# A mixed attention and state-space kernel: two power tables, three chunk-state buffers, parked queries and larger rings for VectorE's exps

## The chip, the cores and the metric

The kernel runs on one core of a Trainium2 chip. The metric is the device time of one execution in microseconds. One execution was also profiled. PE is TensorE, DVE is VectorE, ACT is ScalarE, POOL is GpSimd and SP is SyncE, which here issues nearly all the DMAs.

## What is computed

S = 2048 positions, D = 512 channels, 32 heads of 16. `a` is softmax attention over x, `b` is a state-space convolution of the same input x, and a sigmoid gate mixes the two.

```python
def _A_ref(x, wqkv, wo):
    qkv = (x @ wqkv).reshape(B, S, 3, H, Dh).transpose(2, 0, 3, 1, 4)
    q, k, v = qkv[0], qkv[1], qkv[2]
    p = softmax(einsum("bhqd,bhkd->bhqk", q, k) * Dh ** -0.5)
    return einsum("bhqk,bhkd->bhqd", p, v).transpose(0, 2, 1, 3).reshape(B, S, D) @ wo

def _B_ref(u, A_re, A_im, B_re, B_im, C_re, C_im, log_dt, Dskip):
    dt = exp(log_dt)[:, None]
    P = exp((dt * (A_re + 1j * A_im))[:, :, None] * arange(L))
    K = einsum("dn,dnl,dn->dl", C_re + 1j * C_im, P, dt * (B_re + 1j * B_im)).real
    return causal_convolution(u, K) + u * Dskip        # written with FFTs in the reference

g = sigmoid((x * gate_w).sum(-1, keepdims=True))
out = g * _A_ref(x, wqkv, wo) + (1 - g) * _B_ref(x, ...)
```

The kernel represents each channel's state-space part by powers of one complex number and works in chunks of 64 positions: a power table, the effect within a chunk, the state that a chunk leaves, a scan over chunks, and the output from the states.

## The kernel before

A planner in Python (`record`) writes out the instructions of all five engines. The operations are grouped in generators, called threads (`first`, `projs`, `table`, `scan` and so on), each with a priority; a smaller number goes first. A thread yields operations, or a condition: `AFTER` a mark, `Q` a tile number, or `LOCK` the PSUM bank MB. The planner has a cost for each operation, and at each step it emits what is ready by these costs. On the chip every engine then runs its list in order, with semaphores for dependences. The whole is recorded once, the SBUF addresses are chosen from the first and last use of each buffer (`place`), and the list is emitted.

**Attention** sets the beat. There are 2048 slices of 128 keys by 512 queries of one head, three to a *tile*, so 683 tiles. `fill(t)` is three PE matmuls that write scores into one of two PSUM buffers, SC0 and SC1 (line 572, as all matmuls). `ex(t)` is the exp of a tile on ScalarE (line 725), from PSUM into a ring in SBUF: EX and ET for tiles below TL = 340, EL (9 entries) from there on. `pv` multiplies the exps with the values into the PSUM bank OA; a block of 16 such steps (b, one of 32) ends with `norm` (lines 826 to 832: transpose, reciprocal, product, transpose). Blocks 0 to 7 use the query buffer Q0, 8 to 15 Q1, and so on; `mk_qm` (line 681) makes the masked queries Qm of a block. Matmuls on `wm` keep TensorE's clock up.

**Exps on VectorE.** From tile TL on, `dchoose` may take one slice of a tile away from ScalarE, two slices to a group. `dfirst` (line 736) makes the exponent bits, `dpoly` (lines 756 to 760) makes two correction tensors DP and DC with two maskings and two products. `pv` then adds two more matmuls for that slice. ScalarE's instruction of the tile covers 1024 columns instead of 1536. A new group is begun only if a DP/DC buffer is free (ND = 3), if no other thread has VectorE work ready in the time of the next tile, and if VectorE's backlog by the plan is under DPEND = 2.5 us. The last 40 slices have none.

**The state-space part** runs beside it, in 16 blocks of 32 channels, four blocks to a quarter:

- `table` (lines 983 to 1018): for a pair of blocks, VectorE computes powers into PT from B16 and D16, D32, D48 (12 products, 6 sums, 2 copies), and SP stores PT to DRAM (`ptd`). The next pair waits for `K` of the pair before.
- `kstage` (L1036 to L1044): PE products from PT into MB, VectorE puts them into Kst (L1039, L1041), SP stores to `kpd`, mark `K`.
- `qload` and `sstage` (L1026, L1052 to L1070): SP loads the transposed table into Qt (two buffers), PE multiplies with X2 into MB, VectorE scales into Sst (L1064), SP stores to `sd`. Mark `S`.
- `sload` (L1075 to L1090): SP loads a block's chunk states with a transpose into SG0 or SG1, by the quarter's parity. Quarter 1 waits for the mark `sgfree`, quarters 2 and 3 for `yq0` and `yq1`.
- `scan` (L1093 to L1121): 30 steps a quarter on VectorE, each of two products, an add, the sum into G and a cast back into SG.
- `ystage` (L1142 to L1188): 32 units of PE products from SG, Py, Tt and X2 into MB, a VectorE copy into Yst (L1175), a store to `ytd`. `yread` (L1191) loads the result transposed into Yl. `yq` marks a quarter of it. The thread begins after S15.
- `combine`, `outs` (L1229, L1256): the gate on Yl, the output projection in MB, and the final sum `fo` (L1248).

MB is one PSUM bank and is shared by projections, K, S, y and the output projection, so each of these takes the lock. All DMAs named stand in SP's one queue, in program order.

Of the kernel before, what the change touches and what calls it, by code (L numbers as in the profile page):

```python
# [6 lines left out]
FP32 = mybir.dt.float32  # L7
# [24 lines left out]
ND = 3  # L32
TL = 340
NL = 9
WARM = 2.2
DEBT = 2.5
DPEND = 2.5
DW = ((TL, 9999),)
# [338 lines left out]
def declare(nc, es):  # L377
# [7 lines left out]
    for k in range(4):  # L385
        sb(f"Q{k}", 4 * 512)
    sb("Qm", 2 * 512)
# [3 lines left out]
    sb("EL", NL * 1536)  # L391
# [50 lines left out]
    sb("PT", 2 * 2 * CB * T)  # L442
# [8 lines left out]
    sb("G", 2 * 128, FP32)  # L451
    for n in ("s2", "s3"):
        sb(n, 2 * 128, FP32)

    sb("X2", 4 * 32 * 64)

# [4 lines left out]
    for n in ("DP", "DC"):  # L461
        sb(n, ND * 1024)
# [4 lines left out]
    for n, free in (("ptd", NBLK * P * 2 * CB * T), ("sd", D * NCH * 2 * P),  # L467
                    ("kpd", NBLK * P * 8 * P), ("xrd", S * D), ("ytd", D * S)):
        B[n] = Buf(n, "dr", free, BF16)
        B[n].t = nc.dram_tensor("gm_" + n, [free // P, P], BF16)  # L470
# [7 lines left out]
def place(nc, bufs):  # L478

    base, end = (nc.sbuf_base + 31) // 32 * 32, nc.sbuf_usable_end  # L480
    sbs = [b for b in bufs.values() if b.kind == "sb" and b.first is not None]

    size = {b: (b.nbytes() + 31) // 32 * 32 for b in sbs}
    conf = {b: [o for o in sbs if o is not b and o.first <= b.last + 1 and b.first <= o.last + 1] for b in sbs}

    def fit(order):
        over = 0
        for b in sbs:
            b.lo = None
        for b in order:  # L490
            at = base
            for lo, hi in sorted((o.lo, o.lo + size[o]) for o in conf[b] if o.lo is not None):
                if at + size[b] <= lo:
                    break
                at = max(at, hi)
            b.lo, b.hi = at, at + size[b]
            over += max(0, b.hi - end)
        return over

    seed = 1  # L500

    def rnd(n):
        nonlocal seed
        seed = (seed * 1103515245 + 12345) % 2 ** 31
        return (seed >> 8) % n

    first = sorted(sbs, key=lambda b: -(b.last - b.first + 30) * size[b])
    for k in range(24000):
        if k % 4000 == 0:
            order, best = first, None  # L510
        o = list(order)
        if best is not None:
            x = out[rnd(len(out))] if rnd(10) < 6 else o[rnd(len(o))]
            o.remove(x)
            o.insert(rnd(len(o)), x)
        over = fit(o)
        if best is None or over <= best:
            order, best, out = o, over, [b for b in sbs if b.hi > end]
        if best == 0:
            break  # L520
    assert best == 0, (best, live(sbs))
    fit(order)
# [35 lines left out]
def record(p, B, ins):  # L558
# [109 lines left out]
    def proj_ev(kind, idx, c, bank):  # L668
# [5 lines left out]
        o, at, ky = (KT, idx * S + 512 * c, (idx, c)) if kind == "K" else (B[f"Q{c}"], 512 * idx, idx)  # L674
# [35 lines left out]

    def et(t, n):
        if t >= TL:
            b, e = B["EL"], (t - TL) % NL
        else:
            b, e = (B["EX"], t - NE) if NE <= t < NE + NX else (ET, t % NE)
        return b, 1536 * e + 512 * n, (b, (e, n), t)
# [11 lines left out]
    VC, DP, DC = (B[n] for n in ("VC", "DP", "DC"))  # L728
    groups, gof = [], {}

    def dfirst(t, n):
        b, o, ky = et(t, n)
        sc = SC[t % 2]
        if t >= TL + NL:
            yield ("AFTER", ("pv", tiles[t - NL][n] // 4))
# [12 lines left out]
    def dpoly(g):  # L748
        k = g["n"] % ND
# [14 lines left out]
    def dchoose(t, start, end):  # L764
# [5 lines left out]
        if g is None:  # L770
            if not any(lo <= t < hi for lo, hi in DW):
                return
            if len(groups) >= ND and any(tiles[t_][n_] // 4 >= pvn for t_, n_ in groups[-ND]["t"]):
                return
            if any(isinstance(x[3], list) and x[3][0].eng == "DVE" and (p.ready(x[3]) or 0) < end for x in sch.thr if x[0] > 2.6):
                return
            if NS - sl[-1] < 40 or max(p.free["DVE"], start) + sum({.5: .6, 2.6: 1.9}.get(x[0], 0) for x in sch.thr) > start + DPEND:
                return
            g = dict(n=len(groups), t=[], have=0, op1=[])
# [9 lines left out]
    def vcopy():  # L789
        yield ("Q", DW[0][0] - 5)  # L790
# [4 lines left out]
    def pv(q):  # L795
# [4 lines left out]
        for j in range(4):  # L800
# [7 lines left out]
            if dsel.get(t) == n:  # L808
                g = gof[t]
                k = g["n"] % ND  # L810
                o = 1024 * k + 512 * g["pos"][ek]
                vc = lambda: VC(kt * 152 + 34 * pi + 17 * w, [[1, 32]])
                ext = [main, mm(out, ve, lambda: DP(o, [[1, 512]]), rv + [(DP, k, g["n"])], [(OA, 0, b)], False, False, **kw),
                       mm(out, vc, lambda: DC(o, [[1, 512]]), [(VC, 0), (DC, k, g["n"])], [(OA, 0, b)], False, kt == 15, **kw)]
# [165 lines left out]
    PT, Qt, ptd = B["PT"], B["Qt"], B["ptd"]  # L980
    PTN = 2 * CB * T

    def table():
# [5 lines left out]
        for pb in range(NBLK // 2):  # L989
            qr, blks = pb // 2, (2 * pb, 2 * pb + 1)  # L990
            if pb:
                yield ("AFTER", f"K{2 * pb - 1}")
# [4 lines left out]
            for i in range(2):  # L997
                yield [dv(lambda v, i=i, b0=b0, B16=B16: v.tensor_copy(PT(i * PTN, [[CB * T, 2], [T, CB], [1, 16]]),
                                                                       B16(b0 + i * CB * 16, [[2048, 2], [16, CB], [1, 16]])), bk, [W[i]], 1024, 4)]
            for m in range(1, 4):  # L1000
                Dm = B[f"D{16 * m}"]
                for part in range(2):
# [5 lines left out]
                    yield [tt(lambda part=part, m=m: PT(part * CB * T + 16 * m, [[PTN, 2], [T, CB], [1, 16]]),  # L1008
                              lambda: t1(0, [[CB * 16, 2], [16, CB], [1, 16]]), lambda: t2(0, [[CB * 16, 2], [16, CB], [1, 16]]),
                              ALU.add if part else ALU.subtract, [(t1, 0), (t2, 0)], W, 1024, 2)]  # L1010
            for i, blk in enumerate(blks):
                yield [dma("SP", lambda e, i=i, blk=blk: e.dma_start(ptd.dram(blk * P * PTN, [[PTN, P], [1, PTN]]), PT(i * PTN, [[1, PTN]])),
                           [W[i]], [(ptd, blk)], 6.5, .5)]
                sch.mark(f"pt{blk}")
                if blk == 11:
                    sch.mark("sgfree")
# [3 lines left out]
    X2 = B["X2"]  # L1020
# [9 lines left out]
    def kstage(blk):  # L1030
# [3 lines left out]
        o = (blk % 2) * PTN  # L1034
# [15 lines left out]
    def sstage(blk):  # L1050
        q0, qr, bl = (blk % 2) * PTN, blk // 4, blk % 4
        for bank in range(4):  # L1052
            yield ("LOCK", "MB", [(Qt, blk % 2, blk)])
            os = []
            for pp in range(2):
                for j in range(4):
                    k, par = 4 * bank + 2 * pp + j // 2, j % 2
                    os.append(mm(lambda pp=pp, j=j: MB(256 * pp, [[1, 256]], 32 * j, 32),
                                 lambda k=k, par=par: X2(2048 * qr + 16 * bl + k, [[64, 32]], 64 * par, 64),
                                 lambda k=k, par=par: Qt(q0 + 128 * k, [[16 * 128, 2], [1, 128]], 64 * par, 64),  # L1060
                                 [(Qt, blk % 2, blk), (X2, (qr, par))], [(MB, 0, ('S', blk, bank))], pos=(64 * par, 32 * j),
# [11 lines left out]
    SG = [B["SG0"], B["SG1"]]  # L1073

    def sload(blk):  # L1075
        qr, bl = divmod(blk, 4)
        if qr >= 2:
# [448 lines left out]
```

The softmax here doesn't subtract the row's maximum and nothing guards it: scores larger than these inputs give would overflow.

## Time and profile before

| | us |
|---|---|
| median of 4 runs | 905.72 (903.77 to 906.24) |
| profiled execution's own time | 907.96 |
| its span | 906.2 |
| ScalarE busy | 879.1 (97%) |
| TensorE busy, keep-warm matmuls included | 839.3 (93%) |
| VectorE busy | 806.0 (89%) |
| granted TensorE clock, mean | 0.977 |

The profile's groups give line, engine, operation, output and inputs, shapes and count, then busy time and the mean length of one instruction, then the idle time ahead of it with what ended it. Where instructions of one engine overlap, the mean is longer than busy time over count. A window of the trace gives the busy time of each engine between two times, in microseconds from the span's start.

### The profile page before, as it was taken

The page shows a single profiled execution, that of the slowest core. Times are in us where ns is not written, and L with a number is a line of the kernel's source. Part 1 is how long each engine was busy: PE and PEld are TensorE (multiplying, and loading weights), DVE is VectorE, ACT ScalarE, POOL GpSimd, SP SyncE. Part 2 cuts the span into 40 slices and gives each one's busy share as a digit, 9 for nine tenths or more (in the row PEclk, how much of TensorE's full clock was granted, in tenths as well). Part 3 has the DMA queues.
Part 4 walks back from the last instruction along what each step waited for, and adds up shares of the span by engine and source line. Part 5 has one row for each costly group of instructions (what it writes and reads, how often), then busy time and mean ns, then how long its engine had stood idle before and what let it go on. Part 6 is the DMA issues. An engine that isn't in the chain of part 4 may idle for free.

```text
span 906.2 us, 18586 instructions
## 1 busy us (share of the span) xinstructions
PE 839.3 (93%) x7707; PEld 266.7 (29%) x7707; DVE 806.0 (89%) x1684; ACT 879.1 (97%) x693; POOL 10.3 (1%) x18
## 2 busy tenths in 40 slices
PE   7999999888899889898989999999999999999997
PEld 2222222222222222222223333423323332222222
DVE  7999999997477899999999899999898989999972
ACT  6999999999999999999999999999999999999996
POOL 2000000000000000000000000000000000000000
PEclk9999989999999999999999999999899999999999
DMA  8350000007758568787645658664614311000000
GB/s 197 100 94 1 1 1 1 1 1 209 221 146 210 172 156 219 189 214 197 198 100 131 152 107 187 156 134 105 140 39 103 79 26 36 24 1 1 1 1 24
DMA packets 227412, 92.32 MB, mean 102 GB/s; under 512 B 191872, under 2 KB 215040, under 8 KB 225280
## 3 DMA queue, kind: packets, MB, share of 16 engines
q1 hardware_dynamic: 226128, 90.34, 40.6%
q8 instruction: 61, 1.00, 0.5%
q10 hardware_dynamic: 1200, 0.79, 0.3%
q14 instruction: 23, 0.19, 0.1%
HBM read 27.92 MB, written 35.65 MB: 70 GB/s over the span
## 4 chain that ended last, share of the span: by engine, by line
ACT 63%; PE 29%; DVE 6%; issue 1%; POOL 1%; ACTq 0%; DVEq 0%; POOLq 0%
ACT ET L725 37%; ACT EL L725 23%; PE OA L572 15%; PE SC L572 8%; PE MB L572 5%; ACT EX L725 3%; DVE Sst L1064 1%; DVE G L1114 0%; DVE EL L736 0%; DVE s L1108 0%; DVE s L1112 0%; DVE fo L1248 0%; DVE tt L837 0%; DVE s L1110 0%; DVE SG L1116 0%
## 5 line engine op out<-in xcount | busy, mean ns | idle before, releaser
L725 ACT ACTIVATE ET<-SC 128x1536 bf16<-128x1536 f32 x322 | 435.1, 1684 | 5.7 <-PE SC L572 5.5
L725 ACT ACTIVATE EL<-SC 128x1536 bf16<-128x1536 f32 (+1 forms) x343 | 413.0, 1371 | 5.2 <-PE SC L572 3.9
L572 PE MATMUL SC<-Qm,KT 32*128 32x512 bf16 x2048 | 271.2, 390 | 44.4 <-ACT ET L725 20.3
L572 PE MATMUL OA<-wm 128*128 128x512 bf16 x849 | 264.5, 399 | 1.0 <-DVE wm L631 1.0
L572 PEld LDWEIGHTS SC<-Qm,KT 32*128 32x128 bf16 x2048 | 66.8, 91 | 306.2 <-ACT ET L725 131.5
L572 PE MATMUL OA<-EL,VE 128*32 128x512 bf16 x1028 | 111.2, 392 | 0.1
L572 PE MATMUL OA<-ET,VE 128*32 128x512 bf16 x966 | 98.1, 400 | 0.1
L736 DVE TENSOR_SCALAR EL<-SC 128x512 int16<-128x512 f32 x122 | 82.9, 681 | 13.1 <-PE SC L572 12.3
L572 PEld LDWEIGHTS OA<-wm 128*128 128x128 bf16 x849 | 58.9, 99 | 113.4 <-issue 97.6
L837 DVE TENSOR_TENSOR tt<-B,D 128x1024 bf16<-128x1024 bf16 x96 | 62.8, 685 | 0.5
L1064 DVE TENSOR_TENSOR Sst<-MB,sgn 128x512 bf16<-128x512 f32 x64 | 44.0, 687 | 20.8 <-PE MB L572 20.8
L1114 DVE TENSOR_TENSOR G<-s,s 128x256 f32<-128x256 f32 x120 | 50.7, 423 | 3.3
L1112 DVE TENSOR_TENSOR s<-s,SG 128x256 f32<-128x256 f32 x120 | 50.3, 419 | 0.0
L1110 DVE TENSOR_TENSOR s<-G,MU 128x256 f32<-128x256 f32 x120 | 50.2, 419 | 0.0
L1108 DVE TENSOR_TENSOR s<-G,MU 128x256 f32<-128x256 f32 x120 | 50.1, 418 | 0.0
L572 PE MATMUL OA<-DP,VE 128*32 128x512 bf16 x122 | 46.3, 379 | 0.0
L572 PE MATMUL OA<-DC,VC 128*32 128x512 bf16 x122 | 46.3, 379 | 0.0
L572 PEld LDWEIGHTS OA<-EL,VE 128*32 128x32 bf16 x1028 | 29.6, 94 | 52.0 <-issue 45.5
L837 DVE TENSOR_TENSOR DC<-EL,DP 128x1024 bf16<-128x1024 bf16 x61 | 42.1, 690 | 1.4
L837 DVE TENSOR_TENSOR DC<-DC,DP 128x1024 bf16<-128x1024 bf16 x61 | 41.8, 685 | 0.8
L826 DVE STREAM_TRANSPOSE OT<-OA 128x512 f32<-128x512 f32 x32 | 22.8, 713 | 21.6 <-PE OA L572 21.4
L572 PEld LDWEIGHTS OA<-ET,VE 128*32 128x32 bf16 x966 | 24.7, 94 | 55.2 <-issue 52.4
(148 smaller groups left out, 712.0 us busy)
## 6 DMA issues: line engine op xcount, KB each, us to landing
gm_ptd<-PT SPq DMA_DIRECT2D x16, 1024.0 KB, 6.0
Py<-gm_ptd SPq DMA_DIRECT2D x32, 512.0 KB, 4.5
gm_sd<-Sst SPq DMA_DIRECT2D x64, 128.0 KB, 1.8
gm_kpd<-Kst SPq DMA_DIRECT2D x16, 256.0 KB, 3.9
Tt<-gm_kpd SPq DMA_DIRECT2D x128, 32.0 KB, 3.7
gm_xrd<-in_A_x_dram SPq DMA_DIRECT2D x1, 2048.0 KB, 11.7
X<-gm_xrd SPq DMA_DIRECT2D x8, 256.0 KB, 4.7
gm_ytd<-Yst SPq DMA_DIRECT2D x32, 64.0 KB, 2.2
```

What stands on the lines that cost most here:

```text
L572: return O("PE", lambda t: t.matmul(out(), lhsT(), rhs(), start=start, stop=stop, skip_group_check=True, **kw), R, W, c, l, u)
L725: return ac(lambda a: a.activation(b(o, F), sc(0, F), AF.Exp, scale=LN2 / 128), [(sc, n, (t, n)) for n in ns], [et(t, n)[2] for n in ns], ...
L736: yield [dv(lambda v: v.tensor_scalar(b(o, [[1, 512]]).bitcast(I16), sc(512 * n, [[1, 512]]), -EOFF, EOFF, ALU.max, ALU.add), [(sc, n, (t, ...
L826: yield [dv(lambda v: v.transpose(OT(0, [[1, 512]]), OA(0, [[1, 512]])), [(OA, 0, b)], [(OT, 0, b)], 560)]
L837: return dv(lambda v: v.tensor_tensor(o(), a(), b_(), f), R, W, n, k)
L1064: yield [dv(lambda v, bank=bank: v.tensor_tensor(Sst(512 * bank, [[256, 2], [1, 256]]), MB(0, [[256, 2], [1, 256]]), sgn(0, [[0, 2], [1, 2 ...
L1108: yield [dv(lambda v: v.tensor_tensor(s2(0, V2), G(0, V2), MU(d0, [[0, 2], [1, 128]]), ALU.mult), key("G", "MU"), [(s2, 0)], 256)]
L1110: yield [dv(lambda v: v.tensor_tensor(s3(0, V2), G(128, [[-128, 2], [1, 128]]), MU(D + d0, [[D, 2], [1, 128]]), ALU.mult), key("G", "MU") ...
L1112: yield [dv(lambda v, so=so: v.tensor_tensor(s2(0, V2), s2(0, V2), sg(so, [[RS, 2], [1, 128]]), ALU.add), [(s2, 0)] + ks, [(s2, 0)], 256)]
L1114: yield [dv(lambda v: v.tensor_tensor(G(0, F), s2(0, F), s3(0, F), ALU.add), [(s2, 0), (s3, 0)], [(G, 0)], 256)]
```

## The change

1. `table`: PT becomes PT0 and PT1, used in turn by pairs of blocks. A pair waits for `K` of the pair two before. The mark `sgfree` is set at block 15, not 11.
2. `sload`, `scan`, `ystage`: SG0, SG1 and SG2, by quarter modulo 3. Only quarter 3 waits, for `yq0`.
3. `scan`: two halves of G in turn; the cast of a step is placed between the next step's add and its sum into G.
4. `ystage` begins after S9, at priority 7.5 (6.5 before). `yread` and the load of Wo wait for `yq2`.
5. X2 is four buffers, and those of quarters 1 to 3 are loaded after S1, S5 and S9.
6. The query chunks 2 and 3 are written to Qp2 and Qp3, stored to DRAM after `projs`, and loaded into Q2 and Q3 from tiles 322 and 458.
7. VectorE's exps begin at tile 376 (340 before). The ring is ET up to there, then EL with 11 entries to tile 538, then EM with 14. DP/DC buffers: 4, then 7. Backlog: 4.2, then 5.5 us.
8. `pvs` tests the whole planned length of a PV against the time limit, not 0.33.
9. `place` takes a written order of buffers instead of a search.

```diff
-ND = 3
-TL = 340
-NL = 9
+RINGS = ((24, "ET", NE), (376, "EL", 11), (538, "EM", 14))
+DWS = ((376, 538 - 4, "DPL", "DCL", 4, 4.2), (538, 9999, "DPM", "DCM", 7, 5.5))
-DPEND = 2.5
-DW = ((TL, 9999),)
...
-            if NS - sl[-1] < 40 or max(p.free["DVE"], start) + sum({.5: .6, 2.6: 1.9}.get(x[0], 0) for x in sch.thr) > start + DPEND:
+            if NS - sl[-1] < 40 or max(p.free["DVE"], start) + sum({.5: .6, 2.6: 1.9}.get(x[0], 0) for x in sch.thr) > start + w[5]:
...
+            PT = PTs[pb % 2]
-            if pb:
-                yield ("AFTER", f"K{2 * pb - 1}")
+            if pb > 1:
+                yield ("AFTER", f"K{2 * pb - 3}")
...
-                if blk == 11:
+                if blk == 15:
                     sch.mark("sgfree")
...
-    SG = [B["SG0"], B["SG1"]]
+    SG = [B[f"SG{k}"] for k in range(3)]
...
-        if qr >= 2:
-            yield ("AFTER", f"yq{qr - 2}")
+        if qr == 3:
+            yield ("AFTER", "yq0")
...
+            for r in range(2, NCH):
+                k, o = r % 2, 1 - r % 2
+                yield [tt(lambda o=o: s2(0, V2), lambda o=o: G(256 * o, V2), lambda: MU(d0, [[0, 2], [1, 128]]), ALU.mult,
+                          [(G, o), (MU, 0)], [(s2, 0)], 256)]
+                yield [tt(lambda: s3(0, V2), lambda o=o: G(256 * o + 128, [[-128, 2], [1, 128]]), lambda: MU(D + d0, [[D, 2], [1, 128]]), ALU.mult,
+                          [(G, o), (MU, 0), (MU, 1)], [(s3, 0)], 256)]
+                yield [tt(lambda: s2(0, V2), lambda: s2(0, V2), lambda r=r: sg(2 * RS * r, [[RS, 2], [1, 128]]), ALU.add,
+                          [(s2, 0)] + ks, [(s2, 0)], 256)]
+                if r > 2:
+                    yield [cast(r - 1)]
+                yield [tt(lambda k=k: G(256 * k, F), lambda: s2(0, F), lambda: s3(0, F), ALU.add, [(s2, 0), (s3, 0)], [(G, k)], 256)]
+            yield [cast(NCH - 1, True)]
...
-        yield ("AFTER", "S15")
+        yield ("AFTER", "S9")
...
     def yread(blk):
+        yield ("AFTER", "yq2")
...
-            yield ("Q", 30 + 10 * qr)
+            yield ("Q", 30) if qr == 0 else ("AFTER", f"S{4 * qr - 3}")
...
+            yield [dma("SP", lambda e, c=c: e.dma_start(qd.dram((c - 2) * P * 2048, [[2048, P], [1, 2048]]), B[f"Qp{c}"](0, [[1, 2048]])),
+                       [(B[f"Qp{c}"], i) for i in range(4)], [(qd, c)], 5, .5)]
+
+    def qback():
+        for c, q in ((2, 322), (3, 458)):
+            yield ("Q", q)
...
-            if not must and limit < 1e8 and (r is None or r > p.free["PE"] + .03 or p.free["PE"] + .33 > limit):
+            if not must and limit < 1e8 and (r is None or r > p.free["PE"] + .03 or p.free["PE"] + sum(o.c for o in os) > limit):
```

## The prediction

> **What bounds the kernel now.** I read the page first, then ScalarE's groups by shape, the stretches of time, VectorE's groups by shape, and the order of time inside one scan step.
>
> ```profile
> span 906.2 us, 18586 instructions
> ...
> PE 839.3 (93%) x7707; PEld 266.7 (29%) x7707; DVE 806.0 (89%) x1684; ACT 879.1 (97%) x693; POOL 10.3 (1%) x18
> ...
> DVE  7999999997477899999999899999898989999972
> ACT  6999999999999999999999999999999999999996
> ...
> ACT 63%; PE 29%; DVE 6%; issue 1%; POOL 1%; ACTq 0%; DVEq 0%; POOLq 0%
> ```
>
> ScalarE sets the pace: 97% busy, and most of the chain that ended last. PE's 93% includes 849 keep-warm matmuls that compute nothing. VectorE has the only real hole, slices 10 to 13 (204 to 294 us).
>
> ```profile
> L725 ACT ACTIVATE ET<-SC 128x1536 bf16<-128x1536 f32 x322 | 435.1, 1684 | 5.7 <-PE SC L572 5.5
> L725 ACT ACTIVATE EL<-SC 128x1536 bf16<-128x1536 f32 (+1 forms) x343 | 413.0, 1371 | 5.2 <-PE SC L572 3.9
> ...
> L725 ACT ACTIVATE EL<-SC 128x1024 bf16<-128x1024 f32 x123 | 123.6, 1056 | 0.6 <-PE SC L572 0.2
> ```
>
> A full exp tile costs 435.1/322 = 1.351 us of ScalarE (busy over count; the means overlap). In the EL part 220 full tiles cost 297.2, so the 123 short ones cost (413.0 - 297.2)/123 = 0.941. A 512-column slice that VectorE takes is thus worth **0.41 us of span**. ScalarE's exps run from 14.37 to 897.23 us in the order of time, 873.1 of it busy, 9.8 idle. Span = (span that N = 122 slices gives) - 0.41 x (N - 122) + change of ScalarE's idle.
>
> So the question is how many slices VectorE can take. A pair costs it two L736 (0.681), two L837 products (0.69 + 0.685) and two maskings (0.422 + 0.421): 218.2 us in 61 pairs, **3.58 us a pair**, which saves ScalarE 0.83. VectorE's span: 218.2 pairs, 587.8 everything else, 100.2 idle. Where it idles:
>
> ```profile
> core 0: us, PE busy (x) PEld busy (x) DVE busy (x) ACT busy (x) POOL busy (x), PEclk, DMA share, GB/s
> 0.00:208.00 208.00, 190.87 (x1330) 55.54 (x1330) 195.09 (x298) 199.95 (x154) 5.00 (x11) 0.98 0.20 43
> 208.00:300.00 92.00, 83.36 (x715) 23.89 (x711) 59.36 (x104) 91.39 (x70) 1.23 (x2) 0.98 0.78 212
> 300.00:479.00 179.00, 159.45 (x1411) 47.49 (x1407) 173.04 (x416) 174.78 (x131) 3.35 (x3) 0.95 0.68 176
> 479.00:528.00 49.00, 46.75 (x611) 18.29 (x613) 43.74 (x109) 47.91 (x41) 0.00 (x0) 0.97 0.56 132
> 528.00:655.00 127.00, 119.78 (x1550) 45.74 (x1547) 120.31 (x329) 124.33 (x97) 0.68 (x2) 0.96 0.66 144
> 655.00:883.00 228.00, 222.03 (x2005) 70.70 (x2001) 209.63 (x424) 226.54 (x199) 0.00 (x0) 1.00 0.13 31
> ```
>
> 32.6 us idle in 208 to 300; 5.3 to 18.4 in each later stretch, together 36.3 from 300 to 883. The same query restricted to L736 gives where the 122 exps lie: 12 in 479 to 528, 12 in 528 to 655, 98 in 655 to 883. VectorE exps begin only when its other threads have nothing ready, so idle time anywhere earlier pushes them out.
>
> ```profile
> L736 DVE TENSOR_SCALAR EL<-SC 128x512 int16<-128x512 f32 x122 | 82.9, 681 | 13.1 <-PE SC L572 12.3 <-PE OA L572 0.3
> L1064 DVE TENSOR_TENSOR Sst<-MB,sgn 128x512 bf16<-128x512 f32 x64 | 44.0, 687 | 20.8 <-PE MB L572 20.8
> ...
> L826 DVE STREAM_TRANSPOSE OT<-OA 128x512 f32<-128x512 f32 x32 | 22.8, 713 | 21.6 <-PE OA L572 21.4
> ```
>
> The hole is Sst (17.2 of its 20.8 fall in 200 to 300) and Kst (8.2 us there) waiting for PE, with no table or scan work left to fill in. L736's own wait is for PE's scores. OT's 17.7 us wait is the run's end, where no more exps are allowed; the change leaves that rule alone.
>
> **What the Trainium skill says.** "ScalarE: Activation LUTs", Rules for kernel authors: about 0.83 ns an element, 0.425 us for 512; the trace gives 0.41 and I use that. "VectorE: DVE Perf Modes", The DRAIN you can't avoid: the next op starts only when the pipe is empty, semaphore or not. The trace differs (below: 0.33 us start to start without a dependence, 0.46 with one), and it decides. "Perfetto Trace Analysis", Optimization Strategy: a repeating gap can mean too few buffers; the hole fits. The same page, What "DMA-bound" means: the issuing queue's window is descriptor generation. In the trace a Qt transpose holds SP 5.4 us (median) and lands in 8.0.
>
> **The change part by part**, in VectorE time recovered.
>
> *Two power tables.* The table of pair pb waits for K of pair pb-2, not pb-1. At 208 VectorE has finished pair 0, waits 1.43 and 1.49 us for the K products and 1.66 us for a store, and later runs out again at 228 to 246, 264 to 278 and 278 to 282. A pair's table is 12 products, 6 sums and 2 copies: 62.8 + 33.0 + 6.2 = 102 us in eight. Two more pairs ahead (25 us) fit the hole almost wholly. The scan starts at 299.87, when the fourth SG load lands; S0 to S3 took 213 to 299. A DMA share of 0.78 there allows 92 x 0.78/0.95 = 76 us instead (0.95 is my choice of a full queue). Recovered: 5 us if MB and the queue keep the pace, 28 at most; I take **20**.
>
> *Scan order.* Two float buffers of G, and the cast moved between the add and G.
>
> ```profile
> 309.30 0.42 DVE L1110 TENSOR_TENSOR s<-G,MU 128x256 f32<-128x256 f32 x1
> 309.63 0.42 DVE L1112 TENSOR_TENSOR s<-s,SG 128x256 f32<-128x256 f32 x1
> 310.09 0.42 DVE L1114 TENSOR_TENSOR G<-s,s 128x256 f32<-128x256 f32 x1
> 310.55 0.29 DVE L1116 CAST SG<-G 128x256 bf16<-128x256 f32 x1
> 310.76 0.42 DVE L1108 TENSOR_TENSOR s<-G,MU 128x256 f32<-128x256 f32 x1
> ```
>
> A step is 1.80 us (308.96 to 310.76): 0.34, 0.33, 0.46, 0.46, 0.21. After, the cast follows the add without a dependence, G comes 0.21 later, and only the next product waits: 0.34 + 0.33 + 0.34 + 0.21 + 0.46 = 1.68. 120 steps x 0.12 = 14 at most; where other work already sits in the gap it is nothing. I take **8**. The count of instructions stays.
>
> *Rings of 11 and 14, 4 and 7 coefficient buffers, backlog 4.2 and 5.5 us instead of 2.5.* VectorE may be given pairs ahead, so that a late score tile (12.3 us of waits) or a busy ring does not leave it idle. Of the 36.3 us idle after 300: 0 to 18, I take **10**. The price is that a norm or an MB eviction can stand behind two more ops; 11 or 14 tiles of ring cover it. Two more matmuls per exp of 0.379 us modelled: PE still has 69 keep-warm matmuls in 750 to 850, so nothing.
>
> *No exps between tile 340 and 376* (479 to 528 us at 1.351 a tile). The 12 exps there, 6 pairs or 21.5 us of VectorE, go. With a third SG buffer the scan of quarter 2 no longer waits for yq0 (its loads start at 536.07 now), so scan work fills those 49 us and the pairs come later: **0** if so, -21.5 if not.
>
> *SP's moves.* X2 loads of quarters 1 to 3 go from 51 to 62 us to after S1, S5, S9: six issues of 1.45, 8.7 us of SP inside the S stage, covered since SP waits 81.1 us in all for Sst. Sixteen Yl loads (1.25 us each) and Wo go behind yq2, nothing needs them before the last y. Q2 and Q3: two stores and two loads of 512 KB; Wo, of that size, takes 0.605 of SP and lands in 5.5. Q2 is asked for at tile 322 and used from about 341, 19 x 1.351 = 25.7 us cover. The SG1 gate moves to the last table; SG1 is wanted only after scan 0. One POOL memset more, 0.95 us, idle engine. All zero; uncovered, a late Q2 costs its lateness one for one.
>
> *PV guard.* A PV with VectorE slices is now judged by its whole length, not 0.33 us. It may spare ScalarE some of its 9.8 us idle (0 to 4); I take 0.
>
> *Sum.* 20 + 8 + 10 = 38 us. Recovered time does not convert fully, as a shorter span leaves VectorE less time: 0.83/3.58 = 0.231, over 1.231 = **0.187 us of span per us**. 38 x 0.187 = 7.1: nine pairs net, N about 139 to 140. Span 906.2 - 7.1 = 899.1, own time 907.96 - 7.1 = 900.9, against the median of 905.72: **898.6**.
>
> **Rivals.** *A, nearly all is recovered:* 28 + 14 + 18 = 60 us, 11.2, and 4 off ScalarE's idle: 890.5. For it, every hole has a named cause; against, S is also held by PE's MB bank. *B, the S stage keeps its pace:* only 5 from tables and half of the rest: 14 x 0.187 = 2.6, so 903.1; with none of the rest the change is 1 us, no change to be seen. For it, 17.2 us of the hole is a wait for PE. *C, VectorE starves before tile 376:* the S chain stays as it is, scan 2 does not fill 479 to 528, and the exps barred there are lost: 21.5 x 0.187 = 4.0, **909.7**. It decides once the time left empty ahead of tile 376 exceeds today's by what is won elsewhere (18 us on my values). For it, quarters must still come through one MB bank; against, by volume VectorE has about 535 us of other work before 528 (587.8 less 8 of scan, 29 for 14 late norms with Qm at 2.1, 12 for fo, 4 for Yl) and at most 515 us for it (528 less the 12.9 idle before 208). *D, the tables do nothing*, since the planner's priorities give PE's MB to S first: that is B's number.
>
> **How the numbers follow.** Forecast 0.54 (894 to 903), A 0.20, B and D 0.14, C 0.12. A measurement of this kernel tells 0.2%, 1.8 us: under 903.9 is faster, over 907.5 slower. B splits evenly around 903.9; faster 0.54 + 0.20 + 0.06 = 0.80, same 0.08, slower 0.12. The range 889 to 907 runs from below A to the lower edge of C; the bounds summed without A's idle are 894.5 and (5 - 21.5 = -16.5) 908.8.
>
> **What would show it.** Right: VectorE above 0.85 busy in 208 to 300 (0.65 now); the first G copy before 290; scan step near 1.68; scan 2 running in 479 to 528 with no L736 there; short tiles 135 to 150 instead of 123; L736's wait well under 13.1. Wrong: fewer than 123 short tiles, or ScalarE idle for PE SC much above 10 us, above all near tile 341 when Q2 returns.

## The result and the profile after

The median went from 905.41 us (53 runs, 902.20 to 908.19) to **900.30 us** (34 runs, 895.47 to 907.07). The ratio is 0.9953 with an interval of 0.9941 to 0.9965, so the change takes off 3.2 to 5.3 us; the medians differ by 5.1. The forecast of 898.6 stood for 7.1 us, more than the interval allows. The profiled execution took 903.73 us, with a span of 901.9 (before: 907.96 and 906.2).

The page of the kernel after, the lines that answer to those of before:

```profile
span 901.9 us, 18626 instructions
...
PE 831.3 (92%) x7677; PEld 261.6 (29%) x7677; DVE 831.0 (92%) x1762; ACT 870.4 (97%) x693; POOL 11.2 (1%) x19
...
DVE  7999998999687999999999898999999999999992
...
ACT 54%; PE 34%; DVE 9%; issue 1%; POOL 1%; DMA 0%; ACTq 0%; DVEq 0%; POOLq 0%
```

ScalarE's busy time fell by 8.7 us, but the span by 4.3 only. VectorE has 25 us more work in a shorter span. Its hole is much shallower: slices 11 to 13 read 6, 8 and 7, where slices 10 to 13 read 7, 4, 7 and 7. In the chain, ScalarE's share fell from 63% to 54%, and PE's and VectorE's rose.

The groups of the kernel after, each shape apart (busy time, mean ns of one, idle time before it and what ended it):

```profile
L717 ACT ACTIVATE ET<-SC 128x1536 bf16<-128x1536 f32 x358 | 484.5, 1599 | 12.7 <-PE SC L559 12.5
...
L717 ACT ACTIVATE EM<-SC 128x1024 bf16<-128x1024 f32 x85 | 85.2, 1050 | 0.9
L717 ACT ACTIVATE EL<-SC 128x1024 bf16<-128x1024 f32 x64 | 63.7, 1049 | 0.3
...
L559 PE MATMUL OA<-wm 128*128 128x512 bf16 x764 | 240.7, 400 | 1.0 <-DVE wm L618 1.0
```

```profile
L729 DVE TENSOR_SCALAR EM<-SC 128x512 int16<-128x512 f32 x84 | 57.0, 684 | 2.5 <-PE SC L559 1.5
...
L1060 DVE TENSOR_TENSOR Sst<-MB,sgn 128x512 bf16<-128x512 f32 x64 | 43.8, 684 | 18.1 <-PE MB L559 18.0
L729 DVE TENSOR_SCALAR EL<-SC 128x512 int16<-128x512 f32 x64 | 43.5, 683 | 6.8 <-PE SC L559 6.3
...
L821 DVE STREAM_TRANSPOSE OT<-OA 128x512 f32<-128x512 f32 x32 | 22.8, 712 | 13.7 <-PE OA L559 13.5
...
L1035 DVE CAST Kst<-MB 128x512 bf16<-128x512 f32 x16 | 11.0, 689 | 1.9 <-PE MB L559 1.8
```

Short tiles rose from 123 to 149, and VectorE's exps (L729) from 122 to **148**. Their own wait fell from 13.1 to 9.3 us, and OT's from 21.6 to 13.7 (at the run's end from 17.7 to 13.5). But ScalarE's wait in the ET part, nearly all of it for scores, grew from 5.7 to 12.7, and over all its exps from 11.0 to 15.7 us. The planner has also put fewer keep-warm matmuls: 764 instead of 849, and 325 instead of 345 from 208 to 528 us.

The same stretches of time of the kernel after (columns as before):

```profile
0.00:208.00 208.00, 191.24 (x1326) 55.32 (x1326) 194.85 (x298) 199.49 (x154) 5.00 (x11) 0.98 0.17 41
208.00:300.00 92.00, 82.41 (x705) 23.36 (x701) 75.45 (x138) 89.82 (x68) 1.23 (x2) 0.94 0.86 242
300.00:479.00 179.00, 158.37 (x1506) 48.95 (x1503) 171.95 (x452) 173.97 (x129) 2.55 (x4) 0.94 0.80 189
479.00:528.00 49.00, 42.76 (x569) 16.46 (x568) 46.40 (x131) 44.98 (x34) 2.40 (x2) 0.93 0.81 172
528.00:655.00 127.00, 120.15 (x1619) 46.91 (x1616) 119.77 (x309) 126.54 (x104) 0.00 (x0) 1.00 0.55 129
655.00:876.00 221.00, 215.88 (x1825) 64.48 (x1823) 213.63 (x424) 218.41 (x197) 0.00 (x0) 1.00 0.08 21
```

VectorE is busy 75.5 of 92 us in the old hole (59.4 before). ScalarE stands idle 11.2 us from 208 to 528, where it stood 5.9 before, and gains 2.2 back from 528 to 655. So **the account** of these two profiles is: 8.7 us less work, 4.7 us more waiting of the exps, 4.0 of the 4.3 us of span. The waiting differs from execution to execution: in the two other profiles of the kernel after (`e1_after` and `e3_after` below) the exps wait 16.5 and 12.5 us. The extra waiting lies in the three stretches in which no exp runs on VectorE and the mean clock is 0.93 to 0.94 (0.95 to 0.98 before).

What the change moved in the state-space part shows in three ends: the last table is written at 352 us (436 before), the last step of the scan is done at 609 (674), and the last Sst at 537 (476). VectorE is done with tables and scan earlier, although the S stage itself ends later.

### The profile page after: what moved, and what is told of

It is laid out like the page before. It is cut to its first block, busy times and chain, and to the rows that moved or that the text cites. A ratio compares the mean times of both kernels' runs of the same rounds, so it can differ in the third digit from the quotient of the medians.

```text
span 901.9 us, 18626 instructions
## 1 busy us (share of the span) xinstructions
PE 831.3 (92%) x7677; PEld 261.6 (29%) x7677; DVE 831.0 (92%) x1762; ACT 870.4 (97%) x693; POOL 11.2 (1%) x19
## 4 chain that ended last, share of the span: by engine, by line
ACT 54%; PE 34%; DVE 9%; issue 1%; POOL 1%; DMA 0%; ACTq 0%; DVEq 0%; POOLq 0%
ACT ET L717 35%; PE OA L559 20%; ACT EL L717 12%; PE SC L559 10%; PE MB L559 5%; ACT EM L717 4%; ACT EX L717 3%; DVE s L832 3%; DVE Sst L1060 1%; DVE G L832 1%; DVE SG L1102 1%; DVE EM L729 1%; DVE OT L821 0%; DVE DCM L832 0%; DVE Yst L1175 0%
## 5 line engine op out<-in xcount | busy, mean ns | idle before, releaser
L717 ACT ACTIVATE ET<-SC 128x1536 bf16<-128x1536 f32 x358 | 484.5, 1599 | 12.7 <-PE SC L559 12.5
L717 ACT ACTIVATE EL<-SC 128x1536 bf16<-128x1536 f32 (+1 forms) x162 | 192.9, 1395 | 1.1 <-PE MB L559 0.2
L717 ACT ACTIVATE EM<-SC 128x1024 bf16<-128x1024 f32 (+1 forms) x145 | 162.0, 1228 | 1.9 <-PE SC L559 0.6
L1060 DVE TENSOR_TENSOR Sst<-MB,sgn 128x512 bf16<-128x512 f32 x64 | 43.8, 684 | 18.1 <-PE MB L559 18.0
L729 DVE TENSOR_SCALAR EM<-SC 128x512 int16<-128x512 f32 x84 | 57.0, 684 | 2.5 <-PE SC L559 1.5
L729 DVE TENSOR_SCALAR EL<-SC 128x512 int16<-128x512 f32 x64 | 43.5, 683 | 6.8 <-PE SC L559 6.3
L559 PE MATMUL OA<-EL,VE 128*32 128x512 bf16 x486 | 49.5, 389 | 0.0
L559 PE MATMUL OA<-EM,VE 128*32 128x512 bf16 x434 | 44.3, 389 | 0.2
L559 PE MATMUL MB<-Qt,X 64*32 64x256 bf16 x512 | 29.1, 302 | 13.4 <-DVE Sst L1060 11.5
L1102 DVE CAST SG<-G 128x256 bf16<-128x256 f32 x120 | 36.6, 305 | 0.1
L821 DVE STREAM_TRANSPOSE OT<-OA 128x512 f32<-128x512 f32 x32 | 22.8, 712 | 13.7 <-PE OA L559 13.5
L832 DVE TENSOR_TENSOR ft<-FP,L 128x1024 f32<-128x1024 f32 (+1 forms) x32 | 33.9, 1086 | 0.4
```

Source lines behind the costliest of these rows:

```text
L559: return O("PE", lambda t: t.matmul(out(), lhsT(), rhs(), start=start, stop=stop, skip_group_check=True, **kw), R, W, c, l, u)
L717: return ac(lambda a: a.activation(b(o, F), sc(0, F), AF.Exp, scale=LN2 / 128), [(sc, n, (t, n)) for n in ns], [et(t, n)[2] for n in ns], ...
L729: yield [dv(lambda v: v.tensor_scalar(b(o, [[1, 512]]).bitcast(I16), sc(512 * n, [[1, 512]]), -EOFF, EOFF, ALU.max, ALU.add), [(sc, n, (t, ...
L821: yield [dv(lambda v: v.transpose(OT(0, [[1, 512]]), OA(0, [[1, 512]])), [(OA, 0, b)], [(OT, 0, b)], 560)]
L832: return dv(lambda v: v.tensor_tensor(o(), a(), b_(), f), R, W, n, k)
L1060: yield [dv(lambda v, bank=bank: v.tensor_tensor(Sst(512 * bank, [[256, 2], [1, 256]]), MB(0, [[256, 2], [1, 256]]), sgn(0, [[0, 2], [1, 2 ...
```

## Experiments

All are compared with the kernel before, run beside them. Where the order of buffers in SBUF had to be found anew for an edit, only the list in `place` differs besides.

### What the keep-warm matmuls and the clock do

ScalarE's waits are for PE's scores, so first the suspicion that PE has too much to do. `e1_after` is the changed kernel, on the chip of the three others.

> The changed kernel again, as the base of the runs beside it. In its profile, cut into 4 us pieces from 200 to 544 us, 10.5 of 11.4 us of ScalarE's idle lie in the 13 pieces with a granted clock under 0.9 (4.0 of 6.2 in 9 pieces before). Theory T (the granted TensorE clock dips in the fuller S stage, scores come late, ScalarE waits): 897 to 904, the lower the higher its mean clock; about 0.974 to 0.98. Rival L (the tighter order itself makes scores late, whatever the clock): ScalarE's waits lie evenly, and the time doesn't go with the clock.

It took 897.97 us (895.30 to 906.13), ratio 0.9916 (0.9892 to 0.9941). Its six times go with the mean granted clock of each run: 895.3 at 0.985, 906.1 at 0.972.

`e1_keep_mid` leaves out the keep-warm matmuls of tiles 145 to 375, 325 in all; they compute nothing.

```diff
+            if o.kw and 145 <= prog.q < 376:
+                continue
             prog.put(o)
```

> The changed kernel without the keep-warm matmuls between tiles 145 and 375, about 210 to 528 us; order, exps (148 slices) and all else as planned. T: with less PE work the dips go, clock in 208 to 528 from 0.94 to 0.98 or more, ScalarE's waits for scores fall by 5 to 9 us: 892 to 896. Rival L: the waits stay, since the dropped matmuls stood only where PE had room: 899 to 902. Rival W (the keep-warm matmuls hold the clock up there): clock under 0.9, 910 or more.

It took **905.00 us** (0.9993; 0.9978 to 1.0009), with 149 short tiles still: the gain is gone. Theory T fails; the clock falls as rival W says, but the time stays under its 910. Its stretches of time:

```profile
208.00:300.00 92.00, 78.34 (x612) 17.95 (x612) 75.91 (x136) 91.09 (x69) 1.23 (x2) 0.60 0.84 243
300.00:479.00 179.00, 156.04 (x1367) 38.82 (x1364) 174.25 (x460) 175.65 (x130) 2.55 (x4) 0.54 0.79 189
479.00:528.00 49.00, 44.31 (x525) 13.82 (x514) 46.98 (x131) 45.84 (x34) 2.40 (x2) 0.50 0.81 173
528.00:655.00 127.00, 121.58 (x1547) 45.23 (x1544) 115.47 (x296) 123.03 (x101) 0.00 (x0) 0.92 0.57 126
```

The clock sinks to 0.50 to 0.60, yet PE is about as busy as before in wall time, as each matmul takes longer. ScalarE loses less in 208 to 528 than in the profile of the kernel after (7.4 us against 11.2), but 3.5 us more in 528 to 655. Two more kernels leave keep-warm matmuls out. `e1_keep_all` leaves them out from tile 24 on:

> The changed kernel without any keep-warm matmul from tile 24 on. T: as without those in the middle and 1 to 2 us more from the dips in 100 to 150 us and after 528: 890 to 895. Rival L: 899 to 902. Rival W: clock under 0.9 in the late part, where PE does least real work, 915 or more.

906.99 us, 1.0016 (1.0004 to 1.0028), at a mean clock of about 0.73, and again under rival W's 915. `e1_before_keep_mid` is the kernel before without those of tiles 145 to 375:

> The kernel before without the keep-warm matmuls between tiles 145 and 375; 122 slices on VectorE as before. T: its dips cost 4.0 us of ScalarE idle in 200 to 544, so 2 to 4 us less: 901 to 904, a smaller gain than the changed kernel's. Rival L: no change, 905. Rival W: 915 or more.

910.35 us, 1.0055 (1.0033 to 1.0077). What follows: the keep-warm matmuls can't be spared. Leaving them out gives PE less to do and half the clock together, so it does not show that PE's load is harmless. They earn 7.0 us in the kernel after (905.00 - 897.97) and 5.1 in the one before. The 897.97 rests on six runs; against the ratio of the 34 runs of the kernel after (0.9953) it is 3.6 us.

`e2_fill` goes the other way and adds 88 of them, one behind the first PV of each of the tiles 145 to 389 that has at most one.

```diff
             prog.put(o)
+            if o.more and 145 <= prog.q < 390 and kept[prog.q] <= 1:
+                kept[prog.q] = 99
+                for _ in range(1):
+                    prog.put(o.more())
```

> The changed kernel with 88 keep-warm matmuls more: one behind the first PV of each tile between 145 and 390 that has at most one. Order, 148 slices and all else as planned. Without keep-warm matmuls there the clock fell to 0.5 to 0.6 for good, so the dips are no sign of too much work. Theory G (a dip to half clock follows a thin stretch of PE, such as 218 to 220 and 307 to 309 us, and scores come late while it lasts): fewer dips, mean clock 0.985 or more, 892 to 896. Rival L (PE's order is simply full in that stretch): the added work delays scores further, 900 to 904. If the dips come from waits behind VectorE that the added matmuls don't reach: 897 to 900 at 0.98.

904.42 us (899.27 to 910.33), 0.9988 (0.9969 to 1.0007): no gain, and a higher ratio than the kernel after. Theory G fails, and the time lies just above the range of rival L (900 to 904). With 852 keep-warm matmuls it has about as many as the kernel before, so that their number fell is not what costs the time. In its profiled execution ScalarE is busy all 92.0 us of 208 to 300 and 176.1 of the next 179, at a clock of 1.00 and 0.98. But that can't be put down to the added matmuls, since `e3_after` (below), the changed kernel without them, has it too:

```profile
208.00:300.00 92.00, 81.36 (x725) 23.81 (x725) 78.38 (x142) 92.00 (x70) 1.23 (x2) 1.00 0.88 245
300.00:479.00 179.00, 157.92 (x1574) 50.42 (x1574) 175.30 (x466) 176.81 (x132) 2.55 (x4) 0.97 0.84 192
479.00:528.00 49.00, 43.51 (x559) 16.29 (x559) 45.26 (x126) 43.96 (x33) 2.40 (x2) 0.86 0.73 165
```

479 to 528 in `e2_fill` is as in the kernel after (45.02 against 44.98), and 528 to 655 lost 3.7 us (122.88 against 126.54) in a spell of low clock at 584 to 600. Whether a spell falls in a given place changes from execution to execution of one kernel, so a single profile doesn't show what the added matmuls did there.

### The parts of the change, one undone at a time

**The backlog.** `e2_old_backlog` sets three coefficient buffers and 2.5 us again.

```diff
-DWS = ((376, 538 - 4, "DPL", "DCL", 4, 4.2), (538, 9999, "DPM", "DCM", 7, 5.5))
+DWS = ((376, 538 - 4, "DPL", "DCL", 3, 2.5), (538, 9999, "DPM", "DCM", 3, 2.5))
```

> The changed kernel with the old limits for VectorE's pairs: 3 DP/DC buffers in both parts and a backlog of 2.5 us; rings and all else as changed (SBUF places differ). VectorE takes 134 slices, 14 fewer: by 0.41 us each 5.7 us more than the changed kernel, 903 to 906. My prediction's 10 us of VectorE time would have been 10 x 0.187 = 1.9 us, 899 to 901. If half-clock spells and not the slices decide, the time goes with the clock and the difference is lost in 895 to 907.

903.42 us, 0.9970 (0.9955 to 0.9986), and 135 short tiles instead of 149. L729 waits 18.2 us (9.3 with the backlog) and OT 19.9 (13.7). The time is in the range expected for 14 slices fewer. Against the 34 runs of the kernel after it is less than their price of 5.7 us: the ratios differ by 0.0017, or 1.5 us, with intervals that overlap.

**One table.** `e2_one_table` has one PT and waits for the pair before. To have room, y begins after S12, and Q2 is asked for at tile 333.

```diff
-    PTs, Qt, ptd = (B["PT0"], B["PT1"]), B["Qt"], B["ptd"]
+    PTs, Qt, ptd = (B["PT0"], B["PT0"]), B["Qt"], B["ptd"]
...
-            if pb > 1:
-                yield ("AFTER", f"K{2 * pb - 3}")
+            if pb:
+                yield ("AFTER", f"K{2 * pb - 1}")
```

> The changed kernel with one power table and the old gate (a pair waits for K of the pair before). To fit SBUF the y stage begins after S12, not S9, and Q2 is asked for at tile 333. VectorE takes 128 slices, 20 fewer: 8.2 us, 905 to 908. My prediction's 20 us of VectorE time: 3.7 us, 901 to 904. If the second table's gain is paid back in half-clock spells: ScalarE's waits fall and it comes out within 2 us of the changed kernel, 897 to 901.

912.45 us, **1.0073** (1.0047 to 1.0099), with 129 short tiles. Its stretches of time, and its groups:

```profile
208.00:300.00 92.00, 81.94 (x706) 23.64 (x705) 57.21 (x102) 91.34 (x69) 1.23 (x2) 0.98 0.74 192
300.00:479.00 179.00, 156.34 (x1369) 45.45 (x1367) 155.62 (x374) 174.24 (x131) 4.69 (x5) 0.98 0.84 207
```

```profile
L1060 DVE TENSOR_TENSOR Sst<-MB,sgn 128x512 bf16<-128x512 f32 x64 | 43.8, 684 | 26.7 <-PE MB L559 26.5 <-DMA gm_sd<-Sst 0.2
...
L1035 DVE CAST Kst<-MB 128x512 bf16<-128x512 f32 x16 | 11.0, 688 | 13.5 <-PE MB L559 13.5
```

VectorE idles 34.8 us in 208 to 300 and 23.4 in 300 to 479 (with two tables 16.6 and 7.1); Sst waits 26.7 us for PE (18.1) and Kst 13.5 (1.9). VectorE starves early, as rival C feared: its first exp comes at 640 us (543 with two tables). But the slices alone don't make this kernel so slow. Its 128 are more than the 122 of the kernel before, to which it loses 6.6 us by the ratio, and the loss against the kernel after is more than the 8.2 us of 20 slices. In its profile ScalarE's exps wait 17.0 us (11.0 in the kernel before), about the difference; what makes the scores late there was not looked into. The two small edits beside it were not tried alone.

**The scan's order.** `e2_old_scan` puts the cast behind G again. Exps begin at tile 384 there, for room.

```diff
-                if r > 2:
-                    yield [cast(r - 1)]
                 yield [tt(lambda k=k: G(256 * k, F), lambda: s2(0, F), lambda: s3(0, F), ALU.add, [(s2, 0), (s3, 0)], [(G, k)], 256)]
-            yield [cast(NCH - 1, True)]
+                yield [cast(r, r == NCH - 1)]
```

> The changed kernel with the scan's cast right behind its G, as before; to fit SBUF VectorE's exps begin at tile 384. VectorE takes 144 slices, 4 fewer: 1.6 us, 899 to 902 (my prediction's 8 us of VectorE time: 1.5 us). A step by itself 1.8 us instead of 1.67.

902.38 us, 0.9951 (0.9933 to 0.9969), 145 short tiles: four slices fewer, some of which the later begin of the exps may have cost, and no time that can be told from the kernel after.

### A POOL memset in front of a cast

In the profile after, the largest single wait of ScalarE's exps has its start in one place, in the order of time:

```profile
506.38 2.12 POOL L786 MEMSET VC<- 128x2432 bf16 x1
506.48 2.17 DVE L1102 CAST SG<-G 128x256 bf16<-128x256 f32 x1
...
509.35 0.68 DVE L1060 TENSOR_TENSOR Sst<-MB,sgn 128x512 bf16<-128x512 f32 x1
...
510.18 0.54 PE L559 MATMUL MB<-Qt,X 64*32 64x256 bf16 x8 [2.47 <-DVE Sst L1060]
...
511.31 1.45 ACT L717 ACTIVATE ET<-SC 128x1536 bf16<-128x1536 f32 x1 [2.02 <-PE SC L559]
```

POOL clears VC in 2.12 us. The scan's cast, 0.29 us as a rule, starts 0.10 us later and takes 2.17. Sst stands behind it, PE waits 2.47 us for Sst, the scores stand behind that on PE, and ScalarE waits 2.02, then 1.03. In the kernel before the same memset ran at 435.06 and met no cast. The Trainium skill, "SBUF — State Buffer", SBUF: two separate sides, says that VectorE and GpSimd share a pair of ports: of a GpSimd instruction and a VectorE instruction in a two-port mode, the one that starts first has the pair for its whole length. Whether this cast runs in such a mode the trace doesn't say, but its end agrees: 0.15 us behind the end of the memset. The two other profiles of the kernel after show the same cast (2.16 and 2.17 us) and the same two waits of ScalarE (2.1, then 1.0). A shorter memset does it too: one of 0.94 us for SG at 353.63, of which the change adds one, holds the cast at 354.08 for 0.64 us, again to 0.15 behind its own end.

Four kernels on one chip follow. `e3_after` is the changed kernel again:

> The changed kernel again, as the base of the runs beside it: 896 to 902, with a slope of about -6 us per 0.01 of mean clock.

899.53 us (898.03 to 905.40), 0.9941 (0.9915 to 0.9967). `e3_vc_pads` clears only the 16 columns of each key block that stay zero:

```diff
-        yield [pool(lambda g: g.memset(VC(0, [[1, 16 * 152]]), 0.0), [], [(VC, 0)], 2432)]
+        yield [pool(lambda g: g.memset(VC(136, [[152, 16], [1, 16]]), 0.0), [], [(VC, 0)], 256)]
```

> The changed kernel, but POOL's memset of VC (moved by the change from 435 to 506 us) sets only the 16 columns of each key block that the next instruction leaves (256 elements instead of 2432). In the changed kernel this memset (2.12 us) and a scan cast that starts 0.1 us behind it end together; the cast takes 2.17 us instead of 0.29, Sst behind it is late, PE waits 2.47 us and ScalarE idles 3.05 us in 508 to 516. Theory V (they exclude each other, and this is part of the loss): the cast back at 0.29, PE's wait gone, 2 to 3 us less than the changed kernel beside it. Rival (Sst is late for another reason there): the gap at 508 stays, same time within 1 us.

The same place in the order of time of this kernel:

```profile
500.41 0.31 POOL L786 MEMSET VC<- 128x256 bf16 x1
500.52 0.35 DVE L1102 CAST SG<-G 128x256 bf16<-128x256 f32 x1
...
501.57 0.68 DVE L1060 TENSOR_TENSOR Sst<-MB,sgn 128x512 bf16<-128x512 f32 x1
...
502.40 0.44 PE L559 MATMUL MB<-Qt,X 64*32 64x256 bf16 x8 [0.65 <-DVE Sst L1060]
```

The cast takes 0.35 us (2.16 in `e3_after`), PE's wait is 0.65 instead of 2.47, and ScalarE is busy 46.62 us of 479 to 528 instead of 43.96:

```profile
479.00:528.00 49.00, 43.90 (x594) 17.01 (x594) 45.98 (x134) 46.62 (x35) 0.59 (x2) 0.90 0.81 179
```

The mechanism is shown, and this stretch is 2.7 us better. The whole is 898.56 us, 0.9934 (0.9912 to 0.9957), 1.0 less than `e3_after` by medians, which lies within the intervals (but see the runs at the same clock, below).

`e3_vc_fill` adds to this 66 keep-warm matmuls in tiles 145 to 334, by the rule of `e2_fill`.

> The same, and 66 keep-warm matmuls more, one behind the first PV of each tile between 145 and 334 with at most one (210 to 475 us). With 88 to tile 390 ScalarE's busy time in 208 to 479 rose from 263.8 to 268.1 us, but 479 to 655 lost 3.6. Theory G: keeping only the early ones keeps the gain: 3 to 4 us less than with the pads alone, 891 to 895, clock 0.985 or more. Rival L (each added matmul costs PE time that scores wait for): no gain or 2 us more than with the pads alone.

900.53 us (894.92 to 904.25), 0.9936 (0.9914 to 0.9959): theory G fails again. Its profiled execution had a clock of 0.992 and a span of 893.1, the shortest of all profiles here. ScalarE waited for scores in the ET part 3.6 us, in 11 waits of at most 0.6 (12.5 in 20 in the profile after, at most 2.0). So with the same 149 short tiles and hardly a spell of low clock (3 pieces of 4 us below 0.9 from 200 to 544, 13 in the profile after), an execution comes to 895; but the typical run is not that one. `e3_old_guard` gives a PV 0.33 us again:

```diff
-            if not must and limit < 1e8 and (r is None or r > p.free["PE"] + .03 or p.free["PE"] + sum(o.c for o in os) > limit):
+            if not must and limit < 1e8 and (r is None or r > p.free["PE"] + .03 or p.free["PE"] + .33 > limit):
```

> The changed kernel with the old guard of PV (0.33 us, not its whole length); 148 slices as before. PV with VectorE slices may then delay the next tile's scores: my prediction's 0 to 4 us, 0 taken. If it matters: ScalarE's waits for scores in the EL and EM parts grow from 3 to 5 to 8 us and the time by 2 to 5 us; if not, within 1 us of the changed kernel beside it.

902.37 us, 0.9961 (0.9941 to 0.9980), with as many short tiles. ScalarE's waits for scores in the EL and EM parts are 3.0 us (1.5 in `e3_after`), less than expected. The new guard is worth 2.8 us by medians, 0 within the intervals. No version here beats the changed kernel by more than its interval.

### The runs at the same clock

Most of the scatter between runs of one kernel goes with their mean clock. The 34 runs of the kernel after lie along a line of 5.9 us for 0.01 of clock, with a scatter of 0.9 us around it. Held against this line, the runs of the other kernels lie off it on average by (an estimate; standard errors 0.1 to 0.5 us):

| kernel | mean clock | off the line, us |
|---|---|---|
| `e1_after`, `e3_after` | 0.982, 0.979 | +0.5, +0.6 |
| `e3_vc_pads` | 0.977 | -1.7 |
| `e3_old_guard` | 0.977 | +0.6 |
| `e2_old_scan` | 0.976 | +0.1 |
| `e2_old_backlog` | 0.980 | +3.6 |
| `e2_one_table` | 0.975 | +10.7 |
| `e2_fill` | 0.982 | +7.0 |
| `e3_vc_fill` | 0.986 | +2.9 |

At the same clock the short memset is worth 2.1 us (1.2 to 3.0, with `e3_after` on the same chip), close to the 2.7 of its stretch; the backlog 3.6 us (price of its slices 5.7), the second table 10.7 (8.2), the new guard nothing. The two kernels with added matmuls have a higher clock and not the time that goes with it within one kernel: `e3_vc_fill` is 4.4 us slower than `e3_vc_pads` at the same clock. That fits rival L, and it warns against reading the mean clock as the cause of the time.

## Why the prediction was right, and where its steps were off

**The frame held, one term of it did not.** The forecast was "span that N gives - 0.41 x (N - 122) + change of ScalarE's idle". N came to 148, not 139 to 140: 26 slices, by price 10.7 us instead of 7.1. The third term, which the forecast set to zero, was +4.7 us and took the surplus back. Two errors of opposite sign made the sum come out near. That is luck: nothing in the forecast ties the one to the other.

**The price of a slice** holds late in the run: in 655 to 876 there are 117 short and 80 full tiles in 218.41 us, so (218.41 - 80 x 1.353)/117 = 0.942 a short tile. Yet ScalarE's busy time fell by 8.7, not 10.7. The full tiles have become 1.355 us on average from 1.351 (all exps, less the short tiles at 0.941, by count), 2.0 us in 534 tiles. The waits do that as well. A full tile right behind another adds 1.344 us in both profiles, but one that starts after a gap is busy 1.45 (a short one 1.02 instead of 0.92). 71 exps start after a gap, 46 before; 25 x 0.107 = 2.7 us.

**The terms.** A pair back gives 3.58 x 1.231 = 4.4 us by the prediction's own conversion, so the 13 pairs gained stand for 57 us of VectorE, where 38 were forecast. Undone one at a time:

| term | forecast, us | slices lost without it | by the conversion, us |
|---|---|---|---|
| two tables | 20 (5 to 28) | 20 | 44 |
| backlog, rings | 10 (0 to 18) | 14 | 31 |
| scan order | 8 (0 to 14) | 4 | 9 |

By these runs the first two were mis-sized, each above its upper bound. I bounded the tables by the hole in 208 to 300, but without them VectorE also loses 16 us in 300 to 479. I bounded the backlog by half of the idle time after 300. The three sum to 84, more than 57: the terms overlap, or the barred tiles 340 to 376 cost part of the 21.5 us that I took as zero. The runs don't part these. The 4 slices of the scan agree with its forecast. Its step by itself is, in the order of time of the kernel after:

```profile
570.04 0.76 DVE L832 TENSOR_TENSOR s<-G,MU 128x256 f32<-128x256 f32 x2
570.72 0.42 DVE L832 TENSOR_TENSOR s<-s,SG 128x256 f32<-128x256 f32 x1
571.06 0.29 DVE L1102 CAST SG<-G 128x256 bf16<-128x256 f32 x1
571.26 0.42 DVE L832 TENSOR_TENSOR G<-s,s 128x256 f32<-128x256 f32 x1
571.71 0.76 DVE L832 TENSOR_TENSOR s<-G,MU 128x256 f32<-128x256 f32 x2
```

From 570.04 to 571.71 is 1.67 us (1.80 before, 1.68 forecast). The median step, with other work in its gaps, is 2.00 us in both kernels, so only part of the steps gained.

**The S chain is not faster.** VectorE's 0.82 in 208 to 300 misses the 0.85 named, and the first G copy came at 311.96, not before 290 (299.87 before). Sst still waits 18.1 us for PE (20.8), and the Sst of S3 is done at 299 us (288 before). The second table filled the hole with work; it did not shorten the chain, as rival B said. Only B's price was wrong, since what counts is VectorE's time and not the chain's. The barred tiles were filled with scan and y work: no L729 before 543.0, VectorE busy 46.4 of 49 us in 479 to 528, more than the 43.7 before, and the 12 exps that lay there came later.

**The step that failed** is the cost of PE's and POOL's share: "so nothing" for PE, and "One POOL memset more, 0.95 us, idle engine", by which I passed over what another, older memset would meet once the lists shift. An idle engine is not harmless if it shares something with a busy one. The chain that starts at 506 cost 3.05 us of ScalarE in the profiled run, and 3.1 to 3.2 in the two other profiles of this kernel: it is the part of the added waiting that comes back each time. Most of the rest lies in spells in which the clock is halved. The prediction read 0.98 to 1.00 in the stretches and took it as a given; the check it named, ScalarE's idle for scores "much above 10", came close in the profile after (12.5 in the ET part, 13.1 in all). Q2's return did not do it: the masked queries come at 470.82, and ScalarE runs without a gap from 464.9 to 485.2.

**Where the clock falls.** One-microsecond windows of the kernel after, then the spell:

```profile
218.00:219.00 1.00, 0.72 (x7) 0.20 (x7) 0.97 (x3) 1.00 (x2) 0.00 (x0) 1.00 1.27 290
219.00:220.00 1.00, 0.39 (x3) 0.10 (x3) 1.00 (x2) 1.00 (x3) 0.00 (x0) 1.00 1.27 290
220.00:221.00 1.00, 0.28 (x3) 0.10 (x3) 1.00 (x4) 1.00 (x2) 0.00 (x0) 0.63 0.91 204
221.00:222.00 1.00, 1.00 (x11) 0.14 (x8) 1.00 (x3) 1.00 (x2) 0.00 (x0) 0.50 0.57 129
222.00:227.00 5.00, 5.00 (x21) 1.01 (x18) 3.43 (x6) 3.58 (x4) 1.23 (x2) 0.50 1.17 261
227.00:229.00 2.00, 2.00 (x18) 0.51 (x16) 0.00 (x0) 1.85 (x2) 0.00 (x0) 0.98 1.07 442
```

PE is 0.39, then 0.28 busy for two microseconds; the clock is halved until 227, and ScalarE, which had not waited, loses 1.4 us from 222 to 227 although PE is busy throughout. The same happens at 307 to 315. In between, the four keep-warm matmuls at 223.75 and at 312.44 take 1.89 us together. In pieces of 4 us from 200 to 544, 13 pieces with a clock below 0.9 hold 10.5 of ScalarE's 11.4 us of idle time; before, 9 such pieces held 4.0 of 6.2. The memset's wait lies in one of them too, so the two causes are not apart in this count. The Trainium skill, "TensorE: Matmul & The Clock Gate", Part 1: The HAM clock gate, has half rate after an idle window of about 3.4 us and full rate after a busy one, with a window that runs freely, so that runs differ. The spells here agree in the two rates, 0.50 and 1.00, but PE was not idle so long: the longest gap between its matmuls before the first spell is 0.95 us (219.77 to 220.72). That the thin stretch is what starts a spell is read from their order in time; that keep-warm matmuls hold the clock is shown (`e1_keep_mid`, 0.50 to 0.60 without them); a kernel in which the spells are gone from every run was not found.

## What to carry to other kernels

When an engine with time to spare takes work from the one that sets the pace, cost the receiver in its own time, as here, but then ask what the shifted lists do to the third engine that feeds both: its waits took back half of what ScalarE's shorter work gave. Look through the new order for every long instruction of an "idle" engine that shares a port with a busy one, and make it short rather than hope that it meets nothing. Judge such an edit by many runs, and where their times go with the mean clock, also at the same clock: one profile of 893 and one of 903 came from kernels whose medians could not be told apart, while 2.1 us of the short memset, lost in the medians, show at the same clock.

## What the runs showed of the hardware

- **Within one kernel, time goes with the mean granted clock from run to run.** Over the 34 runs of the kernel after, 5.9 us for 0.01 of mean clock (correlation -0.96), from 895.47 to 907.07 us; for the kernel before 3.7 to 4.3 us on the chips of the experiments (-0.67 to -0.83). From kernel to kernel it does not: `e2_fill` lies 7.0 us above that line. The kernel after also spreads more (11.6 us; the 53 runs of the one before 6.0); that thinner stretches of PE are the reason was not shown.
- **A low clock by itself costs less than that.** Without the keep-warm matmuls in the middle a mean clock of 0.82 costs 4 to 7 us in all. 0.01 of mean clock is 18 us at half rate (0.01 x 900/0.5, an estimate); by the line a third of that would be lost in a spell. A possible reason is that the keep-warm matmuls, at half rate too (four of them 1.89 us at such a place), stand in front of the scores. This was not tried apart.
- **A memset on POOL holds a VectorE cast** until 0.15 us behind its own end: 2.17 us instead of 0.29 beside a memset of 2.12, 0.64 beside one of 0.94, and 0.35 beside one of 0.31.
- **A wait of ScalarE costs more than its own length.** An exp of 128x1536 that starts after a gap is busy 1.45 us; right behind another it adds 1.344.
